# Chunked attention, then a routed feed-forward layer, on one core: h transposed by DMA with a lag of two tiles, the gate on GpSimd, short tiles packed by groups, and later weight loads

## The chip, the core and the metric

The kernel runs on one core of a Trainium2 chip. The metric is the device time of one execution in microseconds (us); lower is better. All arithmetic is float32 at the boundary. PE is TensorE, DVE is VectorE, ACT is ScalarE, POOL is GpSimd, SP is SyncE, which here only issues DMAs; a "q" behind an engine's name (ACTq, SPq) is its instruction queue.

## The reference

Attention runs inside chunks of 64 positions, for batch 8, 8 heads, 576 positions and head width 64. Its output, as 4608 tokens of width 512, is routed to one of 8 experts of hidden width 1024. A token takes the expert of its own largest logit, or, while a local gate is at least 0.5, the expert of the token before it.

```python
scores = scale * np.matmul(q_c, k_c.transpose(0, 1, 2, 4, 3))
attn = np.exp(scores - np.max(scores, axis=-1, keepdims=True))
attn = attn / (np.sum(attn, axis=-1, keepdims=True) + 1e-09)
out = np.matmul(attn, v_c)
...
e = fresh_e if s == 0 or local_gate[b, s] < 0.5 else prev_e
h = np.maximum(x[b, s] @ w1[e], 0.0)
out[b, s] = p[e] * (h @ w2[e])
```

## The kernel before, in words

**Attention** (about the first 165 us) works on 18 tiles of 256 tokens. For each tile PE transposes the paired heads of q and k (L179), forms the scores (L216), transposes the probabilities, multiplies with v (L265), transposes the resulting x and computes the routing logits (L307). SP loads q, k and v and stores x with its logits to `x_d` in device memory (L333). The order of PE, DVE and ACT is written by hand: strings of tokens in `PAR` ("start", "steady" for each iteration, "drain"), which `play` walks. A token such as `tx2*3` issues three atoms of the x transposes of the third tile from the end. Routing of the first 18 columns of 128 tokens happens inside the attention ("hooks"), so that the first three expert tiles ("early" tiles 0 to 2, all of expert 0) can be computed during the drain.

**Expert stage.** Tokens are sorted by expert into tiles of 128 slots. With these inputs 41 tiles (0 to 40) hold tokens. Six are **short**: the first tile of an expert that has at most 64 or at most 32 tokens left over for it (three of each here). For each tile `step(t)` does, on PE: `mm1`, 24 matmuls of 128x512 into h (L666); `x_parts`, four transposes of the next tile's x (L745); `mm2` of the tile before, 24 matmuls into y (L680); `h_parts`, eight 128x128 transposes of this tile's h (L760). Both products run in three passes over a high and a low part of each operand (`PASSES`). ACT copies the high part out of PSUM (L733), DVE subtracts it to get the low part (L734). ACT applies the ReLU (L719). DVE scales y (L792), and POOL scatters it to the output rows (L795). POOL gathers the tile's x rows two tiles ahead (L633).

A short tile skips the split weights: it uses the raw float32 weights of the coming expert, with its rows packed side by side in PE's columns. `mm1_part` (L674) runs 32 or 64 rows by column groups; `mm2_part` (L687) always uses two groups of 64:

```python
for f in fs:
    for j in range(2):
        nc.tensor.matmul(y[HT * j:HT * j + HT, 0:n], hf[:, f % 4, HT * (f // 4):HT * (f // 4) + HT],
                         raw2[f // 2][:, f % 2, n * j:n * j + n], start=(f == 0), stop=(f == 7))
```

When the expert changes, `refill` splits new weights into high (ACT, L105) and low (DVE, L106) parts, four pieces of 128x1024 for w1 and four for w2, and `reload` fetches the weights after them, w1 on the queue of SP and w2 on that of ACT. These branches are chosen at run time from registers that each engine loads. The gate (`prob_atoms`, L650 to L657) is seven small DVE operations and one exponential on ACT for each tile.

**What sets the order.** In the drain and the expert stage PE, DVE, ACT, POOL and SP each run their instructions in the written order, so an instruction that waits holds up all that is behind it on its engine. PSUM tiles: three for transposes, one pair of banks for scores or h, one pair for o or y, one for logits.

Of the kernel before, what the change touches and what calls it, by code (L numbers as in the profile page):

```python
# [8 lines left out]
F32 = mybir.dt.float32  # L9
# [3 lines left out]
U32 = mybir.dt.uint32  # L13
AF = mybir.ActivationFunctionType
ALU = mybir.AluOpType
# [19 lines left out]
QB = (0, EARLY, 8, NTILE)  # L35
# [5 lines left out]
        "z p0*4 t0a*4 t0a t0b*4 t0b t0c*4 t0c t0d*4 t0d p1*4 q3 s0*8 z t1a*4 s0*2 t1a t1b*4 t1b t1c*4 t1c "  # L41
# [20 lines left out]
    "steady": "lq s*8 s h0 tx*8 s va*4 va z1 tq*8 ra*2 h1 tq*8 pr*4 z2 va*4 lv va ra*2 h2 tp*8 s h3 ",  # L62
# [7 lines left out]
def tile_attention_then_moe(ctx: ExitStack, tc, q, k_in, v, wg, wl, w1, w2, out):  # L70
# [133 lines left out]
    def scores(qkT, c, pr, fine=False):  # L204
# [5 lines left out]
        sc = ps_s.tile([P, 2, 4, 2, D], F32, name="sc")  # L210

        def group(h, cc):
            for cp in range(2):
                ch = 2 * cp + cc
                for j in range(2):
                    nc.tensor.matmul(  # L216
                        sc[64 * cp:64 * cp + 64, j, h, cc, :],
                        of(0, j, h, ch),
                        of(1, j, h, ch),
                        start=True, stop=True,  # L220
                    )
# [310 lines left out]
    nc.vector.tensor_scalar(upper, iota_m, pcol, None, ALU.is_gt)  # L532
    zrow = pa1.tile([P, E * NT], F32, name="zrow")
# [617 lines left out]
```

## Time and profile before

| | us |
|---|---|
| median of 3 runs (664.64 to 667.05) | 664.92 |
| the profiled execution, its own time | 665.87 |
| its span, first to last instruction | 664.1 |
| PE busy, of the span | 629.6 (95%) |
| DVE busy | 352.9 (53%) |
| ACT busy | 264.8 (40%) |
| POOL busy | 163.5 (25%) |

The span is cut into 40 slices of 16.6 us on the profile's page; a digit is the busy share in tenths, and PEclk is the granted clock of TensorE in tenths of full speed. The timeline lists instructions in order of time. Consecutive matmuls overlap, so what one costs is read as the distance between starts, not as its own duration. "idle" in brackets is the engine's idle time ahead of the row and what ended it.

### The profile page before, as it was taken

What the parts mean: (1) busy time and instruction counts of PE and PEld (TensorE: products, weight loads), DVE (VectorE), ACT (ScalarE), POOL (GpSimd) and SP (SyncE); (2) the same over time, 40 slices, a digit from 0 to 9 for tenths busy, and PEclk for the clock granted to TensorE, in tenths of its full rate; (3) what the DMA queues carried; (4) which work ended last, traced back from release to release, by engine and by line L of the source; (5) the groups of instructions that cost most, each with busy time, mean ns of one, the idle gap of its engine ahead of it and who ended that gap; (6) DMA issues with size and microseconds to landing.
All of it is one profiled execution on the core that took longest, in us unless ns stands there. A gap on an engine that the chain in (4) does not pass through costs nothing.

```text
span 664.1 us, 16346 instructions
## 1 busy us (share of the span) xinstructions
PE 629.6 (95%) x5667; PEld 500.1 (75%) x5667; DVE 352.9 (53%) x901; ACT 264.8 (40%) x439; POOL 163.5 (25%) x285
## 2 busy tenths in 40 slices
PE   7899999976999999999999999999999999999993
PEld 4678878764677887778888777788876888768872
DVE  2567668773685567662322565732666423564230
ACT  3666767754312244442221353512455222442220
POOL 3434444672141211121211212121122211112101
PEclk7999999989899999999999999999999999999997
DMA  9999999999523114544111154551247511244101
GB/s 215 254 218 275 260 261 240 267 249 315 190 84 123 49 43 168 185 171 166 50 50 35 41 187 162 178 185 34 81 147 279 182 35 35 66 161 170 48 19 38
DMA packets 85421, 98.23 MB, mean 148 GB/s; under 512 B 42388, under 2 KB 61844, under 8 KB 85268
## 3 DMA queue, kind: packets, MB, share of 16 engines
q1 hardware_dynamic: 71236, 61.01, 32.9%
q0 software_dynamic: 6640, 20.65, 9.5%
q10 hardware_dynamic: 7392, 14.68, 6.3%
q8 instruction: 77, 1.26, 0.8%
q14 instruction: 76, 0.62, 0.3%
HBM read 77.28 MB, written 20.35 MB: 147 GB/s over the span
## 4 chain that ended last, share of the span: by engine, by line
PE 45%; issue 27%; DMA 21%; DVE 2%; SPq 1%; POOLq 1%; ACT 1%; POOL 1%; DVEq 0%; ACTq 0%
DMA out<-ysb,sidx 14%; PE y L680 12%; PE h L666 12%; PE tr L179 8%; PE o L265 3%; PE sc L216 2%; DMA qk<-in_k 2%; DMA x_d<-xs 2%; PE tr L760 2%; PE lg L307 1%; SPq L142 1%; PE tr L745 1%; PE y L687 1%; DMA raw<-in_moe_w 1%; PE h L674 1%
## 5 line engine op out<-in xcount | busy, mean ns | idle before, releaser
L680 PE MATMUL y<-w2h,hp 128*128 128x512 f32 x560 | 184.0, 398 | 1.2 <-ACTq L986 1.2
L666 PE MATMUL h<-w1h,xp 128*128 128x512 f32 x560 | 162.0, 399 | 0.0
L795 POOL DMA_INDIRECT out<-ysb,sidx x41 | 41.9, 1021 | 367.2 <-DVE ysb L792 282.0
L680 PEld LDWEIGHTS y<-w2h,hp 128*128 128x128 f32 x560 | 105.2, 188 | 22.8 <-ACTq L986 1.4
L666 PEld LDWEIGHTS h<-w1h,xp 128*128 128x128 f32 x560 | 102.6, 189 | 19.5 <-ACTq L986 0.2
L680 PE MATMUL y<-w2l,hp 128*128 128x512 f32 x280 | 109.3, 390 | 0.0
L666 PE MATMUL h<-w1l,xp 128*128 128x512 f32 x280 | 87.2, 392 | 0.5 <-DVEq L986 0.5
L733 ACT CAST hp<-tr 128x512 fp32r<-128x512 f32 x64 | 34.9, 589 | 118.2 <-PE tr L760 112.6
L792 DVE TENSOR_SCALAR ysb<-y,ppr 128x512 f32<-128x512 f32 x35 | 26.2, 750 | 84.3 <-PE y L680 68.1
L666 PEld LDWEIGHTS h<-w1l,xp 128*128 128x128 f32 x280 | 52.8, 189 | 12.3 <-DVEq L986 1.0
L680 PEld LDWEIGHTS y<-w2l,hp 128*128 128x128 f32 x280 | 52.7, 188 | 10.3 <-DVEq L986 0.3
L719 ACT ACTIVATE hsb<-h 128x1024 f32<-128x1024 f32 x35 | 35.9, 1025 | 58.7 <-PE h L666 55.9
L171 POOL COPY qk<-qk 128x512 f32<-128x512 f32 x69 | 40.0, 614 | 55.4 <-issue 20.6
L734 DVE TENSOR_TENSOR xp<-tr,xp 128x512 fp32r<-128x512 f32 x32 | 22.1, 689 | 58.7 <-ACTq L986 56.1
L734 DVE TENSOR_TENSOR hp<-tr,hp 128x512 fp32r<-128x512 f32 x64 | 41.6, 685 | 16.7 <-ACT hp L733 14.3
L652 ACT ACTIVATE pex<-pex 128x8 f32<-128x8 f32 x41 | 8.6, 210 | 104.6 <-DVE pex L651 92.7
L169 ACT COPY qkT<-tr 128x512 f32<-128x512 f32 x69 | 37.3, 590 | 26.9 <-PE tr L179 26.9
L633 POOL DMA_INDIRECT xg<-x_d,gidx x39 | 40.9, 1048 | 14.1 <-issue 9.8
L179 PE MATMUL tr<-ident,qk 128*128 128x128 f32 x288 | 40.3, 284 | 3.6 <-POOL hot L831 1.6
L179 PEld LDWEIGHTS tr<-ident,qk 128*128 128x128 f32 x288 | 32.0, 144 | 11.9 <-POOL qk L171 5.8
L760 PE MATMUL tr<-ident,hsb 128*128 128x128 f32 x274 | 37.3, 274 | 1.9 <-DVEq L986 1.4
L760 PEld LDWEIGHTS tr<-ident,hsb 128*128 128x128 f32 x274 | 31.9, 140 | 9.6 <-ACTq L986 3.4
(214 smaller groups left out, 802.3 us busy)
## 6 DMA issues: line engine op xcount, KB each, us to landing
raw<-in_moe_w SPq DMA_DIRECT2D x14, 1024.0 KB
raw<-in_moe_w ACTq DMA_DIRECT2D x14, 1024.0 KB, 7.0
raw<-in_moe_w SPq DMA_DIRECT2D x16, 512.0 KB, 4.1
qk<-in_q SPq DMA_DIRECT2D x11, 512.0 KB, 7.4
qk<-in_k SPq DMA_DIRECT2D x11, 512.0 KB, 8.0
v<-in_v SPq DMA_DIRECT2D x22, 256.0 KB, 5.3
x_d<-xs SPq DMA_DIRECT2D x7, 521.0 KB, 9.9
x_d<-x_w2h SPq DMA_DIRECT2D x6, 521.0 KB, 7.4
```

The source lines that it names most:

```text
L169: eng.copy(dst, src)
L171: eng.tensor_copy(dst, src)
L179: nc.tensor.transpose(box["ps"][:, n], src_of(n), ident)
L633: nc.gpsimd.indirect_dma_start(out=dst, out_offset=None, in_=src, in_offset=bass.IndirectOffsetOnAxis(ap=gidx[t].bitcast(U32), axis=0))
L666: nc.tensor.matmul(hs[:, j], xs[a][:, c], W1[w][c][:, 512 * j:512 * j + 512], start=(c == 0 and n == 0), stop=(c == 3 and n == 2))
L680: nc.tensor.matmul(y, hx[f // 4][a][:, f % 4], W2[w][c][:, f % 2, :], start=(f == 0 and n == 0), stop=(f == 7 and n == 2))
L719: nc.scalar.activation(hsb, hs.rearrange("p j f -> p (j f)"), AF.Relu)
L733: nc.scalar.copy(p[:, 0], ps)
L734: V.tensor_tensor(p[:, 1], ps, p[:, 0].bitcast(F32), ALU.subtract)
L760: nc.tensor.transpose(ps[:, n], hsb[:, at + P * n:at + P * n + P], ident)
L792: either(kind and kind[1], lambda: V.tensor_scalar(ysb, y, pr, None, ALU.mult), lambda: y_part(ysb, y, pr))
L795: nc.gpsimd.indirect_dma_start(out=out, out_offset=bass.IndirectOffsetOnAxis(ap=sidx[t].bitcast(U32), axis=0), in_=ysb, in_offset=None, bo ...
```

## The change

- **h turned by DMA.** For a full tile, `planes` copies h out of PSUM as two planes of 16-bit halves, `turn_planes` transposes them with two DMAs on SP's queue, and `join` puts the halves together again, applies the ReLU and splits. This replaces the eight PE transposes for tiles 3 to 38. Short tiles keep PE transposes, now issued with the next x transposes.
- **Lag of two tiles.** `step(t)` runs `mm1(t)`, the x transposes of t + 1, then `mm2(t - 2)`, so that h has two steps to come back. `catch_up` runs the rest ahead of tile 39; tiles 39 and 40 follow the old order, with `mm2` cut in three pieces around the two groups of h transposes. y alternates between two PSUM tiles, and h and the scores use two separate one-bank tiles.
- **Gate on GpSimd** (`pool_probs`): a maximum and a reciprocal stay on DVE, the exponential on ACT, the other steps go to POOL as seven small operations.
- **Gathers** run three tiles ahead.
- **Weights.** w1 is split after the short tile and not before it, all four pieces at once; w2's reload moves from ACT's queue to SP's; the small "lanes" DMAs go.
- **Short tiles by groups.** `mm2_part` uses 128/M column groups with 512 columns each, and `y_part` adds the groups on ACT and DVE.
- **Attention and drain.** The 19 matmuls on ones (`busy`, L510) go. The routing's ranks and one-hots are dealt over more hooks and begin earlier. The w1 split is dealt one piece to an iteration. In the drain the early x transposes (`x0`) and the second half of w2's first load (`l2`) come later, and one `y1` comes ahead of `x3`.

```diff
-        "va2 x0 tp0*4 tp0*4 st*2 va1 tp0 va1 ra3 l2*2 x0 tx2 va1*2 ra3 u*2 tx2 ra3 tx2*2 u*2 ra3 tx2*5 va1 "
+        "va2 tp0*4 tp0*4 st*2 va1 tp0 va1 ra3 tx2 va1*2 x0 ra3 u*2 tx2 x0 ra3 tx2*2 x0 u*2 ra3 l2*2 tx2*5 va1 "
...
-        "p2 m2 x3 y1*2 x3 p1 x3 p2*2 y1 h2 ex l1*3 "
+        "p2 m2 y1 x3 y1 x3 p1 x3 p2*2 y1 h2 ex l1*3 "
...
-    "busy": ((9, 4), {1: (6, 0)}, ()),
-    "hooks": [47, 47, 49, 49, 51, 51, 53, 54, 55, 55, 57, 58, 58, 59, 59, 61, 62, 62],
+    "hooks": [45, 45, 47, 47, 49, 49, 50, 50, 51, 51, 53, 53, 54, 57, 58, 59, 61, 62, 62],
...
+    def mm2_part(hf, y, fs, M):
+        n = P // M
+        per = 8 // n
+        for p in fs:
+            g, k = p % n, p // n
+            f = per * g + k
+            nc.tensor.matmul(y[M * g:M * g + M], hf[:, f % 4, HT * (f // 4):HT * (f // 4) + M],
+                             raw2[f // 2][:, f % 2, :], start=(k == 0), stop=(k == per - 1))
...
+    def planes(hw, hs):
+        for n in range(2):
+            for j, eng in enumerate((nc.scalar, V)):
+                evac(eng, hw[:, j, n], hs[j].bitcast(U16)[:, n::2])
+
+    def turn_planes(hw, ht):
+        for j in range(2):
+            nc.sync.dma_start(ht[:, j].rearrange("p a n t -> p (a n) t"), hw[:, j].rearrange("p a f -> p (a f)"), transpose=True)
+
+    def join(hsb, ht, hp):
...
+        for j in range(2):
+            nc.scalar.copy(bits[:, j, :, :, 1], ht[:, j, 1])
+            V.tensor_copy(bits[:, j, :, :, 0], ht[:, j, 0])
+        for j in range(2):
+            nc.scalar.activation(hp[j][:, 0], full[:, j], AF.Relu)
+            V.scalar_tensor_tensor(hp[j][:, 1], full[:, j], 0.0, hp[j][:, 0].bitcast(F32), ALU.max, ALU.subtract)
...
     def step(t):
+        u = t - 1
+        prc[t], top, below, exp, divs[t] = pool_probs(xgs[t], ehot[:, t])
+        top()
+        hs = new_hs()
+        either(kind[t] and kind[t][2], lambda: [mm1(xps[t], hs, c) for c in range(4)],
+               lambda M: mm1_part(xps[t][2], hs, M), True)
+        hw, ht = planes_of[t] = new_planes(t == TMIN - 1)
+        either(kind[t] and kind[t][1], lambda: planes(hw, hs),
+               lambda M: relu_part(words(hw), hs, M), True)
+        gather_full(t + 3)
+        below()
...
+        xps[t + 1] = x_split(px, kind[t + 1], t + 1 == TMIN)
+        refill(0, t)
+        reload(0, t)
+        if u >= EARLY:
...
+            either(kind[u] and kind[u][1], lambda: join(full, planes_of[u][1], hp),
+                   lambda M: h_short(ph, hf, M, 0, M // 16), True)
+        if kind[t] is None:
+            turn_planes(hw, ht)
+        else:
+            with tc.If(kind[t][3] == 0):
+                turn_planes(hw, ht)
+        flags(t)
...
+            second(t - 2)
+        if t > EARLY:
+            down_y(t - 2)
+        run(exp)
```

The first place is PE in the expert stage, between the last matmul of `mm2` and the next tile's `mm1`. hsb holds h behind the ReLU, tr is the PSUM tile of a transpose; the three transposes of one place are the branches for at most 32 rows, for at most 64 and for a full tile. Before:

```order
L680 MATMUL y<-w2h,hp_4321 128x512
L700 UNCONDITIONAL_BRANCH x3
L986 UNCONDITIONAL_BRANCH
L1007 UNCONDITIONAL_BRANCH
L700 UNCONDITIONAL_BRANCH
L700 COMPARE_AND_BRANCH
L702 COMPARE_AND_BRANCH
L760 MATMUL tr<-ident,hsb 128x128 x2
L702 UNCONDITIONAL_BRANCH
L760 MATMUL tr<-ident,hsb 128x128 x4
L702 UNCONDITIONAL_BRANCH
L760 MATMUL tr<-ident,hsb 128x128 x8
```

Now the same place holds no transposes. They stand behind `mm1`, with the x transposes; hw holds a short tile's h, and the full branch turns x alone:

```order
L686 MATMUL h_4399<-w1h_76,xp 128x512
L728 UNCONDITIONAL_BRANCH
L728 COMPARE_AND_BRANCH
L730 COMPARE_AND_BRANCH
L800 MATMUL tr<-ident,xg 128x128 x4
L823 MATMUL tr<-ident,hw 128x128 x2
L730 UNCONDITIONAL_BRANCH
L800 MATMUL tr<-ident,xg 128x128 x4
L823 MATMUL tr<-ident,hw 128x128 x4
L730 UNCONDITIONAL_BRANCH
L800 MATMUL tr<-ident,xg 128x128 x4
```

The full tile's eight transposes are gone from PE; the short tile's two or four stay.

The second place is SP in the drain. L333 stores x (x_w2h, x_w2l and xs are its buffers), L102 loads halves of w2, L99 quarters of w1. Before:

```order
L333 DMA x_d<-x_w2h 128x2x521 x2
L102 DMA raw_0_85<-in_moe_w 128x2x512 x2
L333 DMA x_d<-x_w2l 128x2x521 x2
L102 DMA raw_1_86<-in_moe_w 128x2x512 x2
L333 DMA x_d<-xs 128x2x521
L102 DMA raw_0_85<-in_moe_w 128x2x512
L99 DMA raw_1_84<-in_moe_w 128x1024
```

Now:

```order
L333 DMA x_d<-x_w2h 128x2x521 x2
L102 DMA raw_0_85<-in_moe_w 128x2x512 x2
L333 DMA x_d<-x_w2l 128x2x521 x2
L333 DMA x_d<-xs 128x2x521
L102 DMA raw_1_86<-in_moe_w 128x2x512 x2
L102 DMA raw_0_85<-in_moe_w 128x2x512
L333 DMA x_d<-xs 128x2x521
```

The two loads raw_1 (two times 512 KB) were ahead of the first store from xs and now stand behind it.

The third place is SP in one step of the expert stage, as it is now. Each pair of loads stands in a branch that is taken when the expert changes:

```order
L1087 DMA raw_0_83<-in_moe_w 128x2x1024
L1087 ISA
L1087 DMA raw_1_84<-in_moe_w 128x2x1024
L1084 UNCONDITIONAL_BRANCH x2
L728 UNCONDITIONAL_BRANCH
L1067 UNCONDITIONAL_BRANCH
L728 UNCONDITIONAL_BRANCH
L1168 COMPARE_AND_BRANCH
L769 DMA_TRANSPOSE ht<-hw 128x8x128 x2
```

The two transposing DMAs of a tile stand behind the reload of w1 on the same queue; before, the two "lanes" DMAs stood there, in the branch that is taken when the expert stays.

## Rows read from the trace of the kernel before

**Rows 1.** The page: busy time by engine, and two lines of the 40 slices.

```profile
PE 629.6 (95%) x5667; PEld 500.1 (75%) x5667; DVE 352.9 (53%) x901; ACT 264.8 (40%) x439; POOL 163.5 (25%) x285
...
PEclk7999999989899999999999999999999999999997
DMA  9999999999523114544111154551247511244101
```

**Rows 2.** Timeline of PE, one full tile: start us, us, instruction, count.

```profile
310.32 0.60 PE L745 MATMUL tr<-ident,xg 128*128 128x128 f32 x4
310.68 0.48 PE L680 MATMUL y<-w2h,hp 128*128 128x512 f32 x1
...
316.25 1.04 PE L760 MATMUL tr<-ident,hsb 128*128 128x128 f32 x8
317.04 0.71 PE L666 MATMUL h<-w1h,xp 128*128 128x512 f32 x2
```

**Rows 3.** Stretches: us, busy PE, PEld, DVE, ACT, POOL, clock, DMA share, GB/s.

```profile
166.00:172.00 6.00, 5.61 (x49) 3.68 (x50) 3.20 (x9) 0.00 (x0) 0.74 (x4) 0.50 0.64 213
310.32:322.60 12.28, 12.28 (x61) 10.23 (x60) 3.94 (x11) 2.78 (x5) 1.98 (x2) 1.00 0.15 46
38.00:134.00 96.00, 92.44 (x2158) 75.68 (x2153) 66.42 (x176) 67.83 (x118) 43.09 (x105) 1.00 1.03 256
```

**Rows 4.** Groups: line, engine, operation, count, busy us, mean ns, idle before.

```profile
L760 PE MATMUL tr<-ident,hsb 128*128 128x128 f32 x274 | 37.3, 274 | 1.9 <-DVEq L986 1.4 <-issue 0.5
L733 ACT CAST hp<-tr 128x512 fp32r<-128x512 f32 x64 | 34.9, 589 | 118.2 <-PE tr L760 112.6 <-DVE ysb L792 2.9 <-PEq L1029 2.6
L734 DVE TENSOR_TENSOR hp<-tr,hp 128x512 fp32r<-128x512 f32 x64 | 41.6, 685 | 16.7 <-ACT hp L733 14.3 <-ACTq L986 1.8 <-issue 0.2
L106 DVE TENSOR_TENSOR w1l<-raw,w1h 128x1024 fp32r<-128x1024 f32 x28 | 33.0, 1221 | 7.9 <-ACT w1h L105 7.9
L654 DVE TENSOR_REDUCE psm<-pex 128x2 f32<-128x16 f32 x41 | 6.9, 169 | 1.3
L510 PE MATMUL tr<-ones 128*128 128x512 bf16 x19 | 7.2, 545 | 1.1 <-DVE ones L513 1.1
```

**Rows 5.** Transfers: issue, count, KB each, median us from issue to landing.

```profile
raw<-in_moe_w SPq DMA_DIRECT2D x16, 512.0 KB, 4.1
x_d<-xs SPq DMA_DIRECT2D x7, 521.0 KB, 9.9
```

**Rows 6.** Timeline of PE around one short tile of at most 32 rows.

```profile
242.81 1.93 PE L674 MATMUL h<-raw,xf 128*32 128x256 f32 x32
244.67 0.66 PE L745 MATMUL tr<-ident,xg 128*128 128x128 f32 x4
...
257.07 3.67 PE L687 MATMUL y<-raw,hf 128*64 128x256 f32 x32
260.68 1.09 PE L760 MATMUL tr<-ident,hsb 128*128 128x128 f32 x8
```

**Rows 7.** Timeline of SP's queue in the drain.

```profile
153.17 0.91 SPq L333 DMA_DIRECT2D x_d<-xs  x1
```

**Rows 8.** Timelines of DVE and PE in the drain, with idle time and its releaser.

```profile
161.16 1.22 DVE L882 TENSOR_TENSOR w2l<-raw,w2h 128x1024 fp32r<-128x1024 f32 x1 [4.19 <-DMA x_d<-x_w2l]
...
165.55 0.69 DVE L279 TENSOR_TENSOR xs<-o,rs 128x512 f32<-128x512 f32 x1 [2.86 <-DMA x_d<-xs]
...
166.39 0.50 PE L265 MATMUL o<-v,pT 64*64 64x65 f32 x8 [5.53 <-DVE xs L321]
```

**Rows 9.** Timeline of PE: four more places where it is idle.

```profile
138.47 0.70 PE L265 MATMUL o<-v,pT 64*64 64x65 f32 x32 [2.44 <-DVE xs L279]
...
200.55 0.63 PE L627 MATMUL tr<-ident,xg 128*128 128x128 f32 x4 [1.24 <-DMA xg<-x_d,gidx]
...
594.74 0.63 PE L760 MATMUL tr<-ident,hsb 128*128 128x128 f32 x4 [1.39 <-DVEq L986]
...
648.39 0.47 PE L680 MATMUL y<-w2h,hp 128*128 128x512 f32 x1 [1.18 <-ACTq L986]
```

More of the change, by code (lines that the diff above doesn't have):

```diff
@@ L13 @@
 U32 = mybir.dt.uint32
+U16 = mybir.dt.uint16
 AF = mybir.ActivationFunctionType
@@ L208, in of @@
             return qkT[64 * j:64 * j + 64, h, at:at + 64]
-        sc = ps_s.tile([P, 2, 4, 2, D], F32, name="sc")
+        sc = [ps_s.tile([P, 4, 2, D], F32, name=f"sc{j}") for j in range(2)]
         def group(h, cc):
@@ L739, in share, with x_turn, x_parts, x_split @@
         V.tensor_copy(dst[:, n:2 * n], ps[:, n:2 * n])
[L741 to L743 removed]
+    def x_turn(xg, ps):
         for n in range(4):
             nc.tensor.transpose(ps[:, n], xg[:, P * n:P * n + P], ident)
+    def x_parts(xg, kind, late=False, own=False):
+        ps = quads()
+        x_turn(xg, ps)
+        return x_split(ps, kind, late, own)
+    def x_split(ps, kind, late=False, own=False):
+        xp = part("xp", "pT" if late else None)
         xf = pc.tile([P, 4, HT], F32, name="xf", **own_tag("xf", own))
@@ L770, in partial, with turned @@
             b = gs[0] * k
-            turn(pss[0], P * b, k)
-            if M == HT:
-                share(hf[:, b:b + k], pss[0][:, 0:k])
-            else:
-                for n in range(k):
-                    dst = hf[:, b + n:b + n + 3:2].rearrange("p q (G d r) -> p G q d r", G=2, d=2)
-                    src = pss[0][:, n].rearrange("p (G q r) -> p G q r", G=2, q=2)
-                    for d in range(2):
-                        evac((nc.scalar, V)[d], dst[:, :, :, d], src)
-        either(kind and kind[0], plain, partial, True)
+            h_turn(hsb, pss[0], P * b, k)
+            h_short(pss[0], hf, M, b, k)
+        def turned():
+            nc.tensor.matmul(pss[0][0:1, 0, 0:1], ones[:, 0:1], ones[:, 0:1], start=True, stop=True)
+            full()
+        either(kind and kind[0], plain if full is None else turned, partial, True)
     def new_ysb(own=False):
@@ L869, in tile_attention_then_moe @@
             store_x(n)
-        for c in {13: (0, 1), 15: (2,)}.get(i, ()):
-            run(w1_split(c))
     early_gather((2,))
@@ L985, in refill @@
         hi, lo, raw = ((w1h, w1l, raw1), (w2h, w2l, raw2))[which]
-        with tc.If(turn[t] != 0):
-            for c in range(3 if which == 0 else 4):
+        with tc.If((fresh, turn)[which][t] != 0):
+            for c in range(4):
                 split(hi[c], lo[c], raw[c])
-            if which == 0:
-                with when(kind[t + 1] and kind[t + 1][1] == 0):
-                    split(hi[3], lo[3], raw[3])
-    lanes = pc.tile([1, 2], F32, name="lanes", bufs=1)
-    turn, fetch = {}, {}
+    turn, fetch, fresh = {}, {}, {}
     def sub(v, engines):
@@ L1033, in when, with down, plain, down_y @@
                     otherwise()
-    kept = []
-    def step(t):
-        tail = t >= TMIN
+    kept, ys, planes_of, divs = [], {}, {}, {}
+    def down(u, cs):
+        y = ys.setdefault(u, None) or new_y(u % 2)
+        ys[u] = y
+        def plain():
+            for c in cs:
+                mm2(hps[u], y, c)
+        either(kind[u] and kind[u][2], plain,
+               lambda M: mm2_part(hps[u][0][2], y, range(2 * cs[0], 2 * cs[-1] + 2), M), True)
+    def down_y(u):
+        keep = u == LAST - 1
+        ysb = new_ysb(u >= LAST)
+        with when(ok[u], (lambda: V.memset(ysb, 0.0)) if keep else None):
+            scale_y(ysb, ys[u], prc[u], kind[u])
+            if not keep:
+                put_y(u, ysb)
+        if keep:
+            kept.append((u, ysb))
@@ new lines, in catch_up, with flags, tail_step @@
+    def catch_up(t):
+        hw, ht = planes_of.pop(t)
+        hps[t], hp, hf = new_hp(t % 2)
+        full = pa2.tile([P, F], F32, name="join", tag="pr")
+        h_parts(words(hw), (0, 1), kind[t], hp, hf, lambda: join(full, ht, hp))
+        second(t - 1)
+        down_y(t - 1)
+        run(divs.pop(t))
+    def flags(t):
+        if t + 2 < NTILE and t + 2 not in kind:
+            kind[t + 2] = kind_of(t + 2)
+        if t + 2 < NTILE:
+            turns(t + 1)
+    def tail_step(t):
+        if t == LAST:
+            with when(ok[t - 1]):
+                down(t - 1, (0, 1, 2, 3))
+            down_y(t - 1)
```

266 lines of the change are left out of this document (149 added, 117 removed), and 4 rows, old and new, of the table PAR.

## The prediction, made before the changed kernel was run

> **What bounds the kernel now.** I began with the page: PE is busy for 95% of the span, the other engines for 53% or less, and the DMA engines are full for the first quarter and then mostly free [rows 1]. A busy PE alone does not prove a bound, so next came the stretches and the timeline. In the expert stage a full tile takes 12.28 us at full clock, with no idle PE, while DVE works 3.94 us, ACT 2.78 us and the DMA share is 0.15 [rows 3]. The timeline splits the 12.28 us: 0.36 for the x transposes, 5.57 for `mm2`, 0.79 for the eight h transposes (317.04 less 316.25), 5.56 for `mm1` [rows 2]. PE's work is the bound there, and every transpose taken off it shortens the tile as long as nobody else gets later than PE. In the attention PE and DMA are both near full (92.4 of 96 us busy, DMA share 1.03) [rows 3], so only idle gaps can be won. In the drain there is one large gap, 5.53 us, behind a store [rows 8], and smaller ones elsewhere [rows 9].
>
> **h transposes: 23.7 us less.** The group of h transposes has 274 records [rows 4]: 32 full tiles of 3 to 40 with 8, three short ones with 4, three with 2, which is 274. The tiles 39 and 40 keep theirs, so 30 full tiles lose eight transposes each. The mean of 274 ns overlaps; the distance of starts is what counts: 30 x 0.79 = 23.7 us. The new full tile is 12.28 - 0.79 = 11.49 us.
>
> What now hides the work: DVE gains two copies of planes and two of the join, at most 0.69 us each by the nearest copy of that size, from PSUM [rows 4], and loses five steps of the gate of some 0.17 us [rows 4], so about 5.9 us of 11.49 (3.94 + 2.8 - 0.85). ACT gains four copies of 0.59 us [rows 4] and loses a little in the ReLU, about 4.5 us. A change of expert adds four low parts of 1.22 us on DVE [rows 4], 4.9 us, in all 10.8 in one step. That is still inside 11.49, and w1's and w2's splits fall in different steps. POOL's small operations have two steps before y needs them. All this costs nothing while it stays hidden; uncovered, one microsecond in each full tile costs 30.
>
> **The transposing DMAs** have no row. A tile moves 2 x 256 KB in two issues on SP. Bounds from rows: a weight load of 512 KB lands after 4.1 us, a store of 521 KB after 9.9 us in a crowded stretch [rows 5]. Below 4.1 us would gain nothing, since it is hidden. Their time is free if a tile's pair is done at a rate of one in 11.49 us; with the lag, its landing may even be some 19 us late (two steps less the planes and the join) before PE waits. I take the range's inside, some 7 us, because the queues are mostly free there (DMA share 0.15), so the price is nothing. Behind the waiting `join` on ACT and DVE stand only the rest of that step and the next planes; behind a waiting SP stand w2's reload and the next transposes. When the expert changes without a short tile, 2 MB of w1 go ahead of the transposes on SP, about 8 us (four times 512 KB by the load row, overlapped), which the 19 us take in; a short tile has no transposing DMA at all.
>
> [...]
>
> **Short tiles: 5.2 us less.** `mm2_part` takes 3.61 us for every short tile (260.68 less 257.07) [rows 6]. For at most 32 rows it now runs in four column groups, as `mm1_part` does, which takes 1.86 us for the same products (244.67 less 242.81) [rows 6]. Three tiles gain 1.75 us each. For 64 rows it stays at two groups. The added sums run on ACT and DVE, hidden.
>
> **Seam and end: 3.1 us less.** The idle 1.24 us ahead of `x3` [rows 9] is covered by the `y1` piece now ahead of it. At the end the last h transposes leave PE idle for 1.18 us [rows 9]; now a quarter of `mm2` stands behind them. The 1.39 us behind DVE [rows 9] comes with the old place of w1's last piece; I take half, 0.7.
>
> **Drain and attention: 6 us less.** The 5.53 us gap ends when x can be normed, which waits for the store issued at 153.17 [rows 7, 8]. Now 1 MB of w2 no longer stands ahead of it. Two loads of 512 KB are worth 2 x 4.1 us at most [rows 5], but a DVE split waits for an older store until 161.16 anyway [rows 8], so the gap can lose about 3 us. [...] A shorter gap may not cure it; I take 1. The 2.44 us gap at 138.47 follows DVE's rank work, which now comes earlier: 2. Bounds are 0, since DMA is full until 165 us, and 10.8 (5.53 + 2.8 + 2.44). The removed matmuls on ones (19, 7.2 us in all [rows 4]) fill idle time while loads arrive; without them the first slice, at 7 tenths of the clock [rows 1], may run slower. I take 0; 2.2 us less if the four between the first scores and the next transposes, 0.545 us each, were on the path, and 3.3 us more if two tenths of the clock go in that slice of 16.6 us.
>
> **Sum.** 23.7 + 5.2 + 3.1 + 6 = 38.0 us. The profiled execution took 665.87 us (span 664.1), 0.95 above the median of 664.92. 665.87 - 38.0 = 627.9; by the median it would be 626.9. I forecast **627 us**. Its own range, 619 to 637, is made of the drain's bounds (6 more, 5 less), the start, and a microsecond of new wait at each of the seven changes of expert.
>
> **The rivals.**
> - *Part is given back.* ACT and DVE get late at the changes of expert: refill stands ahead of `join`, and 10.8 of 11.49 us leaves little. If the copies of 16-bit halves cost twice a float copy, each step with a refill is 2 to 3 us late on w1 and again on w2, 7 x 2 x 1.3 = 18 us: about **645**. For it: the low parts are the longest DVE operations [rows 4]. Against it: pieces are used one after the other, and two steps of lag absorb them.
> - *Nothing is left.* The same lateness with 2.7 us at each of 14 refills is 38 us: **665**, no change. For it speaks only that no row shows the new copies.
> - *Slower: the transposes become the bound.* If the two DMAs of a tile run one after the other and each takes as long as a store of 521 KB, 2 x 9.9 = 19.8 us [rows 5], every full tile takes 19.8 in place of 11.49: 30 x 8.3 = 249 us more, **876**. The point from which it decides is 11.49 + 38/30 = 12.8 us for a tile's pair; at 15 us it would be about 732. For it: two-byte elements and a new kind of transfer. Against it: each moves half as many bytes as that store, and the queues are free there. [...]
> - *The change does not do what it says.* The order of PE excludes that for full tiles: no transposes of h are left in their branch.
>
> **How the numbers follow.** Forecast 0.68, part given back 0.13, no change 0.05, slower 0.12, and 0.02 for a larger gain than the bounds. The range of 8 in 10 takes the forecast's own 619 to 637 and most of the second case: 617 to 650; what it leaves out is no change, slower and the edges. About 0.5%, 3.3 us, is what a measurement of this kernel can tell from no change. Faster by more: 0.68 + 0.13 + 0.02 = 0.83. Within: 0.05. Slower: 0.12.
>
> **What would show it.** Right: full tiles at 11.5 us by the starts of `mm1`, PE without idle time, no transposes from h in full tiles; short tiles of 32 rows with 1.9 us of `mm2`; transposing DMAs that land in under 10 us; the drain's gap at about 2.5 us; the clock at 1.0 through the expert stage. Wrong: PE waiting for hp behind ACT or DVE, whose own releaser is the DMA into ht (slower case) or w1l and w2l (given back); a longer start with a low clock; a drain as long as before. The prediction fails if full tiles take more than 12 us.

## The result, and the profile after

The changed kernel takes **635.89 us** (median of 6 runs, 634.72 to 640.3), the kernel before 664.97 us (6 runs); the ratio is 0.9574 with an interval of 0.9533 to 0.9616. It is 29 us faster, inside the range, and 9 us above the forecast of 627. The profiled execution took 640.15 us (span 638.4), 4.3 above the median.

The page of the changed kernel, the lines that answer to [rows 1]:

```profile
PE 595.9 (93%) x5313; PEld 467.4 (73%) x5313; DVE 378.2 (59%) x813; ACT 318.3 (50%) x546; POOL 263.5 (41%) x559
...
PEclk9998999989998999999999999999999999999997
DMA  9999999998754366597947487969599894559301
```

PE has 34 us less work, the three other engines have 25, 54 and 100 us more, and the DMA engines are 3 to 9 tenths busy through most of the expert stage. The timeline of PE in a full tile, against [rows 2]:

```profile
317.65 0.61 PE L686 MATMUL h<-w1h,xp 128*128 128x512 f32 x2
...
323.10 0.60 PE L800 MATMUL tr<-ident,xg 128*128 128x128 f32 x4
323.45 0.48 PE L700 MATMUL y<-w2h,hp 128*128 128x512 f32 x1
...
329.03 0.62 PE L686 MATMUL h<-w1h,xp 128*128 128x512 f32 x2
```

From `mm1` to `mm1` 11.38 us: `mm1` 5.45, the transposes of x 0.35, `mm2` 5.58. Before it was 12.28. The 0.79 us of h transposes are gone, and `mm1` is 0.11 shorter than the 5.56 it took behind them. One such stretch, columns as in [rows 3]:

```profile
329.03:340.40 11.37, 11.37 (x53) 9.40 (x52) 4.96 (x10) 4.29 (x8) 3.73 (x9) 1.00 0.56 86
```

PE has no gap, DVE works 4.96 us and ACT 4.29, and the DMA share is 0.56. The new groups, and the one that an expert's change adds (columns as in [rows 4]):

```profile
L169 ACT COPY hw<-h 128x512 uint16<-128x512 uint16 x60 | 32.2, 589 | 88.6 <-PE h L686 83.6
L171 DVE COPY hw<-h 128x512 uint16<-128x512 uint16 x60 | 38.6, 685 | 41.2 <-PE h L686 39.9
L775 ACT COPY hsb<-ht 128x512 uint16<-128x512 uint16 x58 | 41.5, 775 | 17.6 <-DMA ht<-hw 8.3
...
L106 DVE TENSOR_TENSOR w2l<-raw,w2h 128x1024 fp32r<-128x1024 f32 x28 | 32.5, 1220 | 15.9 <-ACT w2h L105 13.8
```

Out of PSUM a copy of 16-bit halves costs no more than a float copy of as many elements (ACT 589 and 589 ns, DVE 685 and 691); of the copies that write every second half-word, DVE's takes 461 ns and ACT's 775. The transposing DMAs, all instructions of tile `ht` (duration in ns of the issue on SP, and the time to landing):

```profile
L769 SPq DMA_TRANSPOSE ht<-hw x60: 1231/1358/5005, 214.0 to 586.5; - x60
...
DMA to landing us min/median/max: 3.1/5.1/12.5
```

They land after 5.1 us in the middle, 12.5 at most. The short tile of at most 32 rows, against [rows 6] (`mm2` is L709):

```profile
262.96 1.92 PE L709 MATMUL y<-raw,hf 128*32 128x512 f32 x16
264.71 1.91 PE L694 MATMUL h<-raw,xf 128*32 128x256 f32 x32
266.55 0.66 PE L800 MATMUL tr<-ident,xg 128*128 128x128 f32 x4
267.80 0.50 PE L700 MATMUL y<-w2h,hp 128*128 128x512 f32 x1 [0.60 <-ACTq L1067]
```

`mm2` takes 1.75 us as forecast. But then PE waits: 1.25 us from the transposes of x to `mm2`, because ACT and DVE are not through a branch yet (L1067 is the refill). In the kernel before, the transposes at this place start at 244.67 [rows 6] and `mm2` 0.59 us later:

```profile
245.26 0.50 PE L680 MATMUL y<-w2h,hp 128*128 128x512 f32 x1
```

Such waits stand in the steps of the tiles 9, 10, 22 and 30, at changes of expert. Two more, in the steps of the tiles 3 and 40, stand where no weights are split: there PE waits 1.1 to 1.3 and 0.85 us for DVE to pass the branch of a refill that is not taken.

To see where time goes in each kernel below, each profile is cut at three places of PE: the fourth scoring group (near 31 us), the last one, and the first `mm1` of the expert stage (tile 3), which runs to the end of the span.

| kernel | start | attention | drain to mm1(3) | expert stage |
|---|---|---|---|---|
| before | 30.5 | 111.9 | 62.1 | 459.6 |
| after, first profile | 30.9 | 116.6 | 58.4 | 432.6 |
| after, second profile | 31.4 | 113.6 | 56.1 | 432.5 |
| `pe_turn` | 32.4 | 118.5 | 55.9 | 450.9 |
| `short2` | 30.4 | 110.4 | 56.5 | 432.7 |
| `no_low` | 30.4 | 110.9 | 59.4 | 424.4 |
| `twice` | 30.6 | 112.4 | 57.2 | 458.2 |
| `old_drain` | 32.5 | 111.0 | 62.6 | 431.9 |
| `pool_low` | 30.9 | 109.2 | 57.8 | 468.8 |
| `gate_dve` | 31.9 | 113.7 | 58.4 | 447.2 |
| `planes_act` | 32.6 | 115.7 | 59.0 | 433.8 |
| `join_first` | 31.3 | 114.3 | 56.5 | 457.1 |
| `pe_turn_gate` | 32.1 | 115.2 | 55.9 | 451.0 |
| `end_put` | 31.4 | 112.6 | 55.7 | 433.8 |

The expert stage repeats better than the attention (109 to 119 us with the same code). The two profiles of the changed kernel agree to 0.1 us there, but by luck: `mm1` of tile 3 to `mm1` of tile 38 takes 372.2 and 371.4 us, the rest 60.4 and 61.1. With `old_drain` and `end_put`, whose edits lie elsewhere, these two parts take 371.4 to 373.1 and 59.8 to 61.1. So a few microseconds in the expert stage are read from this table, not from the totals, and a difference under 2 us is not read at all. The change gives 27 us in the expert stage and some 2 in front of it.

### The profile page after: what moved, and what is told of

The parts are those of the page before. It is cut to its first block, busy times and chain, and to the rows that moved or that the text cites. A ratio compares the mean times of both kernels' runs of the same rounds, so it can differ in the third digit from the quotient of the medians.

```text
span 638.4 us, 16143 instructions
## 1 busy us (share of the span) xinstructions
PE 595.9 (93%) x5313; PEld 467.4 (73%) x5313; DVE 378.2 (59%) x813; ACT 318.3 (50%) x546; POOL 263.5 (41%) x559
## 5 line engine op out<-in xcount | busy, mean ns | idle before, releaser
L686 PE MATMUL h<-w1h,xp 128*128 128x512 f32 x560 | 158.8, 393 | 0.1
L169 ACT COPY hw<-h 128x512 uint16<-128x512 uint16 x60 | 32.2, 589 | 88.6 <-PE h L686 83.6
L171 POOL COPY qk<-qk 128x512 f32<-128x512 f32 x69 | 40.2, 617 | 60.9 <-issue 31.3
L171 DVE COPY hw<-h 128x512 uint16<-128x512 uint16 x60 | 38.6, 685 | 41.2 <-PE h L686 39.9
L179 PE MATMUL tr<-ident,qk 128*128 128x128 f32 x288 | 43.7, 299 | 10.9 <-ACT qk L169 5.5
L169 ACT COPY qkT<-tr 128x512 f32<-128x512 f32 x69 | 37.6, 589 | 30.5 <-PE tr L179 25.1
L775 ACT COPY hsb<-ht 128x512 uint16<-128x512 uint16 x58 | 41.5, 775 | 17.6 <-DMA ht<-hw 8.3
L627 POOL DMA_INDIRECT xg<-x_d,gidx x39 | 45.6, 1170 | 9.5 <-issue 4.4
L779 DVE SCALAR_TENSOR_TENSOR hp<-hsb,hp 128x512 fp32r<-128x512 f32 x58 | 37.6, 690 | 14.4 <-ACT hp L778 14.4
L106 DVE TENSOR_TENSOR w2l<-raw,w2h 128x1024 fp32r<-128x1024 f32 x28 | 32.5, 1220 | 15.9 <-ACT w2h L105 13.8
L778 ACT ACTIVATE hp<-hsb 128x512 fp32r<-128x512 f32 x58 | 33.5, 623 | 10.1 <-DVE hsb L776 9.0
L227 DVE TENSOR_REDUCE mx<-sc 128x8 f32<-128x512 f32 x36 | 23.1, 684 | 22.5 <-PE sc L216 22.5
```

Source lines behind the costliest of these rows:

```text
L106: (lo_eng or nc.vector).tensor_tensor(lo, raw, hi.bitcast(F32), ALU.subtract)
L169: eng.copy(dst, src)
L171: eng.tensor_copy(dst, src)
L179: nc.tensor.transpose(box["ps"][:, n], src_of(n), ident)
L627: nc.gpsimd.indirect_dma_start(out=dst, out_offset=None, in_=src, in_offset=bass.IndirectOffsetOnAxis(ap=gidx[t].bitcast(U32), axis=0))
L686: nc.tensor.matmul(hs[j], xs[a][:, c], W1[w][c][:, 512 * j:512 * j + 512], start=(c == 0 and n == 0), stop=(c == 3 and n == 2))
```

## The experiments

Twelve runs follow. The diffs show the lines that matter; "..." marks places where changed lines are left out.

### again: is the long front of the first profile part of the change?

> The changed kernel once more. Theory: the 2.35 us in which PE stands in the middle of a scoring group at 47 us, with nothing in the profile that it waits for, and the low clock behind it are an accident of the profiled execution (it took 640.15 us, 4.3 above the median). Then this profile has no such gap there, the first full tile's mm1 starts at 201 to 202 us and not at 205.8, and the span is 633 to 635 us. Rival: the gap belongs to the change, since the scores now lie in two tiles; then it stands at the same place again, and mm1 starts near 205.8.

Measured: 636.23 us, ratio 0.9564 (0.9524 to 0.9604), span 633.6, `mm1` of tile 3 at 201.11. The gap at 47 us is gone, as the theory had it. But others of its kind are there, the longest in the timeline of PE (`sc` is a scoring group, cut in the middle):

```profile
132.85 1.15 PE L216 MATMUL sc<-qkT 64*64 64x64 f32 x60
...
136.74 0.48 PE L216 MATMUL sc<-qkT 64*64 64x64 f32 x4 [2.74 <-issue]
```

Sixty matmuls of a group of 64 run, PE stands for 2.74 us, and nothing that the profile shows releases it. In thirteen profiles with this front such pauses before tile 3 add up to 0.3 to 7.4 us, 3.6 in the mean; the one profile of before has 1.7. The four profiles with under 2 us of them take 109.2 to 112.4 us for the attention, the four with over 6 us take 113.6 to 118.5. Whether the change makes them more frequent stays open, with one profile of before.

### pe_turn: the same order, but PE turns h

```diff
-        either(kind[t] and kind[t][1], lambda: planes(hw, hs),
+        either(kind[t] and kind[t][1], lambda: relu(words(hw), hs),
...
+            def both():
+                x_turn(xgs[t + 1], px)
+                h_turn(words(planes_of[u][0]), ph, 0, 4)
+                h_turn(words(planes_of[u][0]), ph2, 512, 4)
...
-            either(kind[u] and kind[u][1], lambda: join(full, planes_of[u][1], hp),
+            either(kind[u] and kind[u][1], lambda: (split4(ph, hp[0]), split4(ph2, hp[1])),
```

> The changed kernel with its order and its lag of two tiles, but h is turned by PE again (eight transposes per full tile, between the transposes of x and mm2), and there are no transposing DMAs, planes or joins. Theory: the gain of the expert stage is PE's work that is gone. Then a full tile takes 12.2 to 12.3 us again, 30 x 0.79 to 30 x 0.92 = 24 to 28 us more, some 660 to 664 us. Rival: the lag of two tiles and the new order make the gain; then the time stays within 10 us of the changed kernel, at or below 646.

Measured: 655.32 us, ratio 0.9844 (0.9798 to 0.9891), 19 us more than the changed kernel. Full tiles take 12.25 us, as the theory said, but the sum is smaller than 24 to 28. The two stretches from `mm1` of tile 3 to the end, `again` first:

```profile
201.11:633.60 432.49, 415.28 (x2024) 323.53 (x2023) 243.33 (x440) 205.04 (x349) 168.77 (x332) 0.99 0.62 151
```

```profile
206.82:657.70 450.88, 438.69 (x2263) 348.86 (x2262) 180.29 (x320) 164.14 (x289) 148.78 (x330) 0.99 0.32 110
```

PE has 23.4 us more work, but 5 us less idle time (12.2 against 17.2): DVE is freed of 63 us, and the waits at the changes of expert go. Of the 5 us, 3.4 are such waits between matmuls; 1.7 lie behind PE's last matmul, where profiles differ by as much (10.4 to 12.4 us). So turning h by DMA brings 18 us net in this stage: 23 in PE's work, 5 paid back. The other 9 us between `pe_turn` and the kernel before (450.9 against 459.6) belong to the rest of the change; the three short tiles' `mm2`, 1.75 us shorter each, are a part, and the others were not taken apart. The rival, that order alone makes the gain, is out.

### short2: short tiles of 32 rows in two groups

```diff
...
-               lambda M: y_part(ysb, y, pr, M), True)
+               lambda M: y_part(ysb, y, pr, HT), True)
...
-               lambda M: mm2_part(hps[u][0][2], y, range(2 * cs[0], 2 * cs[-1] + 2), M), True)
+               lambda M: mm2_part(hps[u][0][2], y, range(2 * cs[0], 2 * cs[-1] + 2), HT), True)
```

The lines left out copy h a second time for the wider groups, 0.3 us on each of ACT and DVE.

> The changed kernel, but mm2 of a short tile of at most 32 rows runs in two column groups, as for 64 rows. Theory: three tiles lose 1.75 to 1.8 us each, 5.3 us more, some 641 us. Rival: the three tiles lie at changes of expert, where PE waits for the refilled weights anyway, so that part of the gain is given back there; then only 1 to 3 us more, 637 to 639.

Measured: 635.15 us, ratio 0.9558 (0.9516 to 0.96). No difference, and the expert stage is 432.7 against 432.5: not the theory's 5.3, and not to be told from the rival's lower end. PE's timeline, with `mm2` of a short tile at L709:

```profile
254.21 3.65 PE L709 MATMUL y<-raw,hf 128*64 128x512 f32 x16
257.79 1.93 PE L694 MATMUL h<-raw,xf 128*32 128x256 f32 x32
```

`mm2` is 1.83 us longer in each of the three tiles. Against `again` the steps of the tiles 8, 11 and 20 are 1.9, 1.7 and 1.6 us longer, those of 9, 10 and 22 are 1.5, 1.3 and 1.3 shorter: their waits are gone. Two things do that. PE arrives later, and the second pair of sums over groups is left out too. In the changed kernel it stands on ACT and DVE just ahead of the refill (`again`):

```profile
264.48 0.68 DVE L742 TENSOR_TENSOR ysb<-ysb,y 64x512 f32<-64x512 f32 x1 [1.84 <-ACT ysb L741]
265.80 0.68 DVE L745 TENSOR_TENSOR ysb<-ysb,y 32x512 f32<-32x512 f32 x1 [0.65 <-ACT y L744]
```

The first cast of w1 begins 6.9 us behind the start of the short tile's `mm1` in `again` and 4.1 here; 1.3 of these 2.8 us are the sums. So the four groups' gain is eaten partly because PE comes sooner to a wait, partly by sums that the prediction called hidden; the two were not run apart.

### no_low: a change of expert without the low parts

```diff
-                split(hi[c], lo[c], raw[c])
+                nc.scalar.copy(hi[c], raw[c])
```

> The changed kernel without the low parts of w1 and w2 at a change of expert (eight subtractions of 1.16 us per change on DVE are left out; the low parts stay those of the first expert). Theory: the waits of PE at the changes of expert, some 8 us in sum in the profile, come from DVE, whose refill of 4.6 us stands ahead of the join and of the branches; then they shrink to 1 to 3 us, and the time falls by 5 to 7 us, to 629 to 631. Rival: they come from ACT and from weights that land late behind the transposing DMAs; then at most 2 us less, 634 or more.

Measured: 628.39 us, ratio 0.9444 (0.9409 to 0.9479), 7.8 us less. The expert stage:

```profile
200.66:625.10 424.44, 412.72 (x2024) 322.89 (x2023) 178.16 (x384) 202.44 (x349) 146.94 (x331) 0.99 0.63 154
```

DVE has 65 us less, the stage is 8.1 us shorter. Of these, 4.6 lie in the steps of the tiles 9, 10, 22, 30 and 31, at changes of expert, as the theory has it. The step of tile 3 is 1.4 us shorter and PE's last steps 1.2, though no low part is made there. In `again`, PE at tile 3:

```profile
201.11 0.73 PE L686 MATMUL h<-w1h,xp 128*128 128x512 f32 x2
202.98 0.73 PE L686 MATMUL h<-w1l,xp 128*128 128x512 f32 x2 [1.14 <-DVEq L1067]
```

PE waits for DVE's skipped branch before it uses `w1l`. In this run DVE writes no `w1l` in that branch, and the second row follows `mm1`'s start at 200.66 without a wait:

```profile
201.23 0.63 PE L686 MATMUL h<-w1l,xp 128*128 128x512 f32 x2
```

The last 0.8 lie behind PE's end, which varies by more. So the low parts themselves cost 4.6 us, and 2.6 belong to the branch. Full tiles away from a change keep their 11.37.

### gate_dve: the gate back on VectorE

```diff
-        G = nc.gpsimd
+        G = nc.vector
```

> The changed kernel with the gate's small operations on VectorE again, in the same places of the program. Theory: DVE is what PE waits for at the changes of expert alone; six or seven operations of 0.15 to 0.2 us more per tile are hidden in full tiles and add 1 us at some of the changes, 2 to 6 us more, 638 to 642. Rival: they are hidden everywhere; then within 1.5 us of the changed kernel, 634.5 to 637.5.

Measured: 652.59 us, ratio 0.9828 (0.9783 to 0.9873): **16 us more**, over twice the upper end of what I expected. The timeline of DVE at one change:

```profile
401.18 0.15 DVE L670 TENSOR_TENSOR pex<-pex,ehot 128x8 f32<-128x8 f32 x1
401.40 0.37 DVE L665 TENSOR_TENSOR pex<-pex 128x8 f32<-128x8 f32 x2
...
403.30 0.28 DVE L678 TENSOR_SCALAR pex<-xg,pm 128x8 f32<-128x8 f32 x1 [0.47 <-issue]
403.53 0.69 DVE L791 TENSOR_TENSOR xp<-tr,xp 128x512 fp32r<-128x512 f32 x1
404.14 1.21 DVE L106 TENSOR_TENSOR w1l<-raw,w1h 128x1024 fp32r<-128x1024 f32 x1
```

and PE beside it, with the stretch behind its wait:

```profile
402.78 0.80 PE L686 MATMUL h<-w1h,xp 128*128 128x512 f32 x2
405.41 0.77 PE L686 MATMUL h<-w1l,xp 128*128 128x512 f32 x2 [1.83 <-DVE w1l L106]
```

```profile
405.41:409.81 4.40, 4.40 (x12) 3.48 (x13) 4.06 (x5) 1.73 (x4) 0.00 (x0) 0.61 0.57 172
```

From 401.18 to 403.58 nine small operations of the gate, two of which are on DVE in the changed kernel too, hold DVE for 2.4 us with 1.6 us of work, ahead of x's low part and of `w1l`. PE, which has both other operands, waits 1.83 us for the first low part; then the granted clock is 0.61 in the 4.4 us that follow, so that the wait is paid nearly twice, if the low clock is put down to it. The steps of the tiles 9 and 10 are 2.7 us longer together than in `again`, those of 22 and 31 by 2.7 and 3.6, those of 12 and 24 by 1.6 each; steps away from a change are the same. In the steps of 12, 24 and 31 it is not a low part that is late but DVE's copy of planes, which has to empty h's PSUM before the next `mm1`:

```profile
511.39 0.49 PE L686 MATMUL h<-w1h,xp 128*128 128x512 f32 x1 [2.14 <-DVE hw L171]
```

So undoing the move of the gate, to which the prediction gave no price, takes back more than half of the change's gain.

### pe_turn_gate: does the gate matter when DVE has no joins?

The edits of `pe_turn` and `gate_dve` together.

> The run in which PE turns h again (655.3 us), now with the gate on VectorE too. With the transposing DMAs the gate's place is worth 16 us (652.6 against 636.2). Theory: it is worth that only since the copies of planes and the join have taken VectorE's slack; without them VectorE is idle for half of each tile and the gate is hidden: within 3 us of 655.3. Rival: the gate's small operations delay VectorE's refill by themselves; then 8 to 16 us more, 663 to 671.

Measured: 656.13 us, ratio 0.9847 (0.9791 to 0.9903), against 0.9844 for `pe_turn`; the expert stage is 451.0 against 450.9. The theory holds: the gate's place is worth nothing while PE turns h, and 16 us when the DMAs do. Read the other way, turning h by DMA wins 3.8 us of the expert stage while the gate is on DVE (451.0 to 447.2), and 18.4 with it on GpSimd (450.9 to 432.5). The two parts of the change work only together.

### pool_low: half of the low parts on GpSimd

```diff
-                split(hi[c], lo[c], raw[c])
+                split(hi[c], lo[c], raw[c], nc.gpsimd if c in ((1, 3), (1, 3))[which] else None)
...
```

The lines left out let GpSimd read the registers that choose the branch.

> The changed kernel with half of the low parts of w1 and w2 at a change of expert (the second and fourth of four) on GpSimd in place of VectorE. Theory: DVE is late at the changes, by 4.6 us of low parts ahead of the join; with half of them gone half or more of the 8 us that leaving them all out gave are won, 4 to 6 us less, 630 to 632. Rival: GpSimd takes 2.5 us per low part and is needed for gathers, stores and the gate, so that PE now waits for it; then no gain or a loss, 635 or more.

Measured: 671.65 us, ratio 1.0153 (1.0102 to 1.0204): 35 us slower than the changed kernel. My hope failed, and the rival's side holds, by more than its words. The timeline at two changes, `w1l` on both engines and the wait of PE:

```profile
234.99 4.75 POOL L106 TENSOR_TENSOR w1l<-raw,w1h 128x1024 fp32r<-128x1024 f32 x2
235.49 5.33 DVE L106 TENSOR_TENSOR w1l<-raw,w1h 128x1024 fp32r<-128x1024 f32 x1 [0.67 <-ACT w1h L105]
...
272.61 4.66 POOL L106 TENSOR_TENSOR w1l<-raw,w1h 128x1024 fp32r<-128x1024 f32 x2
274.99 1.22 PE L686 MATMUL h<-w1l,xp 128*128 128x512 f32 x2 [3.54 <-POOL w1l L106]
```

Two things are seen. POOL comes to its part late, behind gathers, a store and the gate (272.61, when PE has begun `mm1` at 269.47); waits for POOL's `w1l`, up to 4.7 us each, or for POOL's branch behind it make up two thirds of all that PE waits in this stage. And subtractions of DVE were drawn out beside POOL's: the one from 235.49 lasts until 240.82, 1.08 us after POOL's two have ended at 239.74, where it takes 1.2 us alone. Five of DVE's 28 are drawn out like this.

### planes_act: one copy of planes from DVE to ACT

```diff
-            for j, eng in enumerate((nc.scalar, V)):
+            for j, eng in enumerate((nc.scalar, V if n else nc.scalar)):
```

> The changed kernel with one of VectorE's two copies of planes per full tile on ScalarE (three copies there, one on VectorE). Theory: VectorE is what PE waits for at the changes of expert, and it alone; 0.69 us less of it per tile gives back a part of the 8 us, 2 to 4 us less, 632 to 634. Rival: ScalarE, whose four casts at a change come ahead of VectorE's low parts, is as late, and 0.59 us more of it costs as much or more; then 636 to 642.

Measured: 639.23 us, ratio 0.9594 (0.9545 to 0.9643), not to be told from the changed kernel; the expert stage is 1.3 us longer, which is within its scatter. The step of tile 10 gets 1.3 us shorter, that of 9 gets 2.1 longer, where profiles of the same code agree to 0.2. The gain that the theory asked for is not there. The rival fits better: ACT's casts and DVE's low parts are one chain, and work moved from one to the other comes back.

### join_first: the refill behind the join

In a step `refill(0, t)` and `reload(0, t)` stand behind the block of the join in place of ahead of it.

> The changed kernel with the join of a tile's transposed halves ahead of the refill of w1 in a step, as the prediction's second case names the refill's place ahead of the join as the cause of lateness. Theory: the place is the cause; with the join first mm2 never waits for it, and the refilled parts come one by one as mm1 takes them (1.16 us for a part, 1.36 us for its matmuls); 2 to 5 us less, 631 to 634. Rival: it is the sum of VectorE's work in a step, not its place; then mm1 waits for w1l instead, 0 to 15 us more, 636 to 651.

Measured: 657.96 us, ratio 0.9876 (0.983 to 0.9922): 22 us more. PE at a change:

```profile
273.93 0.73 PE L686 MATMUL h<-w1h,xp 128*128 128x512 f32 x2 [2.03 <-ACT w1h L105]
275.22 1.22 PE L686 MATMUL h<-w1l,xp 128*128 128x512 f32 x2 [0.56 <-DVE w1l L106]
```

`mm1` now waits, first for ACT's cast, then for DVE. The refill's place ahead of the join is right, and the prediction's second case had the cause wrong: what makes PE late is how much ACT and DVE have to do in such a step, as `no_low` shows for DVE.

### twice: the slack of the transposing DMAs

```diff
...
+        if more:
+            again = pa1.tile([P, 2, 2, 4, P], U16, name="again", tag="v0")
+            for j in range(2):
+                nc.sync.dma_start(again[:, j].rearrange("p a n t -> p (a n) t"), hw[:, j].rearrange("p a f -> p (a f)"), transpose=True)
...
```

> The changed kernel, with each full tile's two transposing DMAs from tile 7 on issued a second time into a spare tile that nobody reads (27 full tiles). Theory: what bounds them is the time of the DMA engines. In a full tile without a weight load the DMA share is 0.55 of 11.37 us, and 0.15 of 12.28 us before, so a pair takes (6.25 - 1.84) = 4.4 us of all engines; two pairs and the rest fill 10.7 of 11.37 us, the share rises to about 0.95, and the time stays within 10 us. Rival, the slower case of the prediction: transposes run one behind the other, each as long as its landing of 5.1 us; then four take 20.4 us per tile, 27 x 9 = 240 us more, some 880 us.

Measured: 659.79 us, ratio 0.9915 (0.9875 to 0.9954): 24 us more, neither 10 nor 240. A full tile without a change keeps 11.37 us, with four transposes in it, at this share:

```profile
330.00:341.00 11.00, 11.00 (x52) 9.16 (x51) 4.97 (x10) 4.33 (x8) 4.12 (x12) 1.00 0.84 148
```

The share is 0.84, not the 0.95 expected. So in a full tile a pair could take twice its time. Of the loss, 22 us stand in the steps of the tiles 20, 23 and 30, at changes, where 2 MB each of w1 and w2 share the queues and SP issues them behind the transposes. At tile 30:

```profile
513.93 1.94 PE L709 MATMUL y<-raw,hf 128*64 128x512 f32 x3 [7.57 <-ACT hsb L779]
```

PE waits 7.6 us for ACT's join, and ACT had waited 3.0 and 2.4 us for weights and 2.0 us for a transpose just before. The changed kernel is not bound by transposes, but at a change twice as many are too many. Whether SP's time to issue them or the DMA engines' time decides that was not tried.

### old_drain: the drain's old order

```diff
-        "va2 tp0*4 tp0*4 st*2 va1 tp0 va1 ra3 tx2 va1*2 x0 ra3 u*2 tx2 x0 ra3 tx2*2 x0 u*2 ra3 l2*2 tx2*5 va1 "
+        "va2 x0 tp0*4 tp0*4 st*2 va1 tp0 va1 ra3 l2*2 x0 tx2 va1*2 ra3 u*2 tx2 ra3 tx2*2 u*2 ra3 tx2*5 va1 "
```

The line ahead of this one gets back its `x0` at the end.

> The changed kernel with the old places of w2's second half and of the first tile's transposes in the drain (w2's two loads again ahead of the waiting vectors). From the last scores to the first full tile's mm1 the kernel before takes 62.1 us, the changed one 58.4, 56.1, 56.5, 59.4 and 55.9 in five profiles. Theory: the order of the drain makes this difference; then the stretch is 60 to 63 us again, the gap of 5 us behind the store is back, and the time is 3 to 5 us longer, 639 to 641. Rival: the difference comes from the routing and the split of w1 that are now dealt into the attention; then the stretch stays at 56 to 59 us and the time within 2 us.

Measured: 640.6 us, ratio 0.9661 (0.9619 to 0.9704), 4.4 us more, and 62.6 us from the last scores to `mm1` of tile 3, where twelve profiles with the new order have 55.7 to 59.4, 57.2 in the mean. The theory holds for the time. The gap of 5 us behind the store is not back, though; PE waits elsewhere than in the kernel before:

```profile
151.79 0.70 PE L265 MATMUL o<-raw,pT 64*64 64x65 f32 x32 [2.70 <-DVE xs L279]
...
155.50 1.09 PE L621 MATMUL tr<-ident,raw 128*128 128x128 f32 x4 [2.76 <-DMA raw<-x_d,gidx]
```

```profile
150.00:160.00 10.00, 5.45 (x69) 3.84 (x69) 3.61 (x9) 4.99 (x9) 1.31 (x2) 0.68 0.89 325
```

Two waits of 2.7 us, and a granted clock of 0.68 with them (`again` has 1.00 in these 10 us and 7.64 us of work).

### end_put: the last store ahead of the branch

The loop over `kept` stands ahead of the last branch.

> The changed kernel with the store of the last tile that always exists issued ahead of the skipped branch for further tiles, and not behind it. In the profile of the changed kernel that store starts 1.75 us after its rows are ready (629.70 against 627.95), behind a branch on GpSimd that waits until the store before it has landed; in the kernel before the delay is 0.27 us. Theory: the new cut of the last mm2 makes the store before it later, and the branch passes that on to the end; issued ahead of the branch, the store starts within 0.4 us of its rows, and the end comes 1.0 to 1.5 us sooner, some 635 us. Rival: the store itself waits for the one before it; then nothing changes.

Measured: 638.61 us, ratio 0.9597 (0.9544 to 0.9651), no gain. The end of the changed kernel, and that of `end_put`:

```profile
627.20 0.75 DVE L864 TENSOR_SCALAR ysb<-y,ppr 128x512 f32<-128x512 f32 x1 [5.83 <-PEq L1102]
629.70 0.97 POOL L868 DMA_INDIRECT out<-ysb,sidx  x1 [6.58 <-DVEq L1102]
```

```profile
621.99 0.75 DVE L864 TENSOR_SCALAR ysb<-y,ppr 128x512 f32<-128x512 f32 x1 [5.80 <-PEq L1102]
623.52 0.97 POOL L868 DMA_INDIRECT out<-ysb,sidx  x1 [5.57 <-DVEq L1067]
```

The store starts 0.8 us behind its rows in place of 1.75, but the span ends 10.1 us after that start, not 8.7. Something behind the store sets the end; what, stays open. None of the variants beats the changed kernel while computing all of it.

## Why the prediction was right, and which terms were not

The sign, the range and the main mechanism held. The forecast was 9 us too low: 3.7 of them in the expert stage (27.1 gained, 30.8 expected) and some 5 in front of it (about 2 gained, 7.2 expected).

- **h transposes, 23.7 forecast.** Right in kind. A plain full tile gains more than forecast, 12.28 - 11.37 = 0.91 us, since `mm1` itself, which doesn't follow transposes of h now, is 0.11 shorter (5.45 against 5.56); 30 of them would be 27 us. But undoing it costs 18 in this stage (`pe_turn`), since the waits at the changes come with it. Full tiles at 11.5 us and no idle PE in them: as written. Landings under 10 us: 5.1 in the middle, but 12.5 at most.
- **"All this costs nothing while it stays hidden", 0 forecast: the step that failed.** I held 10.8 us of DVE against 11.49 of PE in one step and called it hidden. At a change PE's order is short (a short tile's `mm1` and `mm2`, 1.8 us each, come next to it) and DVE's parts are wanted one after the other from the step's start. The low parts cost 4.6 us at the changes (`no_low`), and the new sums of the short tiles stand ahead of them (`short2`). The plain step was not the fault: DVE works 4.96 us there, where I had 5.9. The case "part is given back" had the mechanism at 18 us; its cause, the refill's place, is refuted by `join_first`.
- **The gate, 0.85 us less DVE per tile, no price.** It is worth 16 us (`gate_dve`), and nothing without the joins (`pe_turn_gate`). A term booked at nothing was the cover of the largest term. My own sum held it: without the 0.85 the 10.8 us of such a step are 11.65, over the 11.49 of PE. That the forecast came out inside its range was luck in this: with the gate left on VectorE the time is 652.59, outside 617 to 650.
- **Short tiles, 5.2 forecast.** `mm2` got shorter by 1.75 to 1.83 us as forecast, but undoing it, with its sums, costs nothing that can be measured (`short2`): PE arrives sooner at a wait, and the sums, booked as hidden, make ACT and DVE later.
- **Drain, 3 and 1, and the seam, 1.24.** 62.1 to 57.2 in the mean, 4.9 us, and 62.6 with the old order: the sum is right, and the drain's order makes it. The gap of 5.53 us is down to waits of 0.3 to 2.9, and the granted clock of the whole stretch rises from 0.93 to 0.97 in the first profile. No run shows the 1 us that I took for the low clock behind the gap, or the 2.8 of its bound; what is shown in their place is this clock. The seam gave little: the wait of 1.24 ahead of `x3` is 0 to 0.9 now, but one of 1.0 for DVE stands ahead of the `y1` piece in all thirteen profiles.
- **Attention, 2 for the gap of 2.44, and the start, 0.** Not seen in the time. The gap itself is gone: PE's waits with a known cause in the attention fall from 4.9 us to 3.1 in the mean. But thirteen profiles take 113.4 us in the mean against 111.9, with 2 us more of pauses that nothing in the profile explains, and the start takes 31.5 against 30.5 in the one profile of before. Whether the removed matmuls cost that 1 us was not tried.
- **End, 1.18 and 0.7.** The wait of 1.39 that I halved is gone whole. PE's last stretch is 0.5 us shorter: its wait of 1.18 is gone, but one of 0.85 for a skipped branch stands there now. And the last store starts 2.7 us after PE's end in place of 1.1, behind the landing of the store before it (628.46 in the chain that ended last), which the new cut of `mm2` makes later: 1 us lost. That this is the cause is argued from the chain of waits; `end_put` did not settle it.
- **Slower, by transposes as a bound.** Refuted: full tiles keep their 11.37 us even with twice the transposes, at a DMA share of 0.84 (`twice`). The case took 9.9 us, a store's time, for each of a tile's two DMAs, one behind the other; here a DMA lands in 5.1 us in the middle.

## What to carry to other kernels

Cost the helpers of a removed step where the most other work meets them, not in the mean tile: a busy share of 59% hid the step that decided 16 us. When work goes from the bounding engine to another, look at once for what else that other engine can give away, and undo each part alone and together: here two parts were worth 4 us and nothing apart from each other and 18 together, and a third, right by its own term, nothing that could be measured. When an edit removes work, look where the time comes back: 2.6 of the 8 us of `no_low` came from a branch and not from the work. Read small gains from steps that repeat, and learn from several profiles how well they do.

## What the runs showed of the hardware

In the places shown here, where a DVE subtraction of two operands in SBUF and operations of POOL ran side by side, one of the two took longer than alone. In `pool_low` a subtraction of 1.2 us took 5.33 beside two of POOL, which took 4.75 together there and 4.66 from 272.61, where DVE subtracts no low part. In the changed kernel it is the other way round; the timeline of POOL at a change and in a plain tile:

```profile
321.56 0.48 POOL L665 TENSOR_TENSOR pex<-pex 128x8 f32<-128x8 f32 x2
...
400.58 2.21 POOL L665 TENSOR_TENSOR pex<-pex 128x8 f32<-128x8 f32 x2
```

The same two additions take 2.21 us while DVE subtracts low parts, four in 4.63 us. Why the one takes longer, no trace shows. It fits that the gate does well on POOL, where its pieces of 0.2 to 0.33 us can wait, and the low parts do not.

A wait of PE of 1.83 us was followed by 4.4 us at a granted clock of 0.61 (`gate_dve`), one of 3.54 us by 0.50 in the next 5.3 us (`pool_low`):

```profile
274.99:280.28 5.29, 5.29 (x13) 4.13 (x13) 0.00 (x0) 0.00 (x0) 4.01 (x6) 0.50 0.79 287
```

A wait of 1.14 us in `again`, at tile 3, was followed by 4.0 us at 1.00:

```profile
202.98:207.00 4.02, 4.02 (x18) 3.33 (x19) 1.87 (x5) 0.00 (x0) 2.15 (x4) 1.00 0.25 79
```

So the short wait cost its own length. The two longer ones cost 1.9 and 1.7 times theirs, if all of the low clock behind them is put down to them.
